# Queueing side work behind each slot's ELU, and making three weight tiles of the second MoE in place

## The chip, the cores and the metric

The kernel runs on one core of one Trainium2 chip. The metric is device time in microseconds (us) of one launch. Before the change the median of three runs is 1340.48 us (1339.67 to 1345.49).

## The reference, cut to what matters

Three layers follow each other: attention with pooled keys and values (8 batches, 8 heads, 576 queries of 64), a first MoE block with ELU (4608 tokens, 512 to 2048 to 512), and a second one with SoLU and a layer norm (512 to 1024 to 512).

```python
k_p = k.reshape(B, H, Sp, 8, D).mean(axis=3); v_p = ...          # pooled by 8
x = softmax(q @ k_p.T / 8) @ v_p                                  # 4608 x 512
h = x @ w_in                                                      # 512 -> 2048
g = np.where(h > 0.0, h, np.exp(np.minimum(h, 0.0)) - 1.0)        # ELU
x = g @ w_out                                                     # 2048 -> 512
h = x @ w_in2                                                     # 512 -> 1024
solu = h * softmax(h)
out = ((solu - mean) / sqrt(var + 1e-6) * g_ln) @ w_out2          # 1024 -> 512
```

## The kernel before

Every float32 operand of a matmul is split into a rounded high part and a low remainder, and three products (high by high, low by high, high by low) are added; the high part is a copy on ScalarE (ACT), the remainder a subtraction on VectorE (DVE). The weights come as 64-bit words and are converted by bit operations on ACT and DVE. A scheduler orders the instructions of each engine by when it believes they can run; the source's order decides among those that are ready.

The first MoE works on nine blocks of 512 tokens, in two ways.

Blocks 0, 1 and 2 are **three passes** of 16 *slots* (the loop over `slots`, j for the block, f for 128 columns of the hidden layer). A slot holds 12 matmuls of `m_h1` (line 529, into a bank `h`), ELU on ACT and DVE (`m_h1` lines 534 and 535 for the exponentials, `m_elu` line 541 on DVE, the copy `gh` at 545, the remainder `gl` at 552), and 12 matmuls of `m_o1` (line 564) for the slot before. Side work is sown into the slots: attention for later blocks (`att_half`, four steps for each *unit*, a pair of heads of one batch: scores 173, their maximum and difference 189 and 198, exponentials 203, sums 212 to 214, the multiplication on GpSimd 216, transposes 228 and 233 on TensorE, the product 252), and from block 1 on the *combinations* of the weights (`combo_in`, `combo_out`, the generator `todo`), which make sums of quarters of the weights for the third stage: DVE subtractions at 469, ACT copies at 474, remainders at 478, writes to DRAM (`w1d`, `w3d`) at 481. The tiles `ci` and `co` of the combinations, the blocks `xh`, `xl` and, later, the `sP`, `sA`, `sV`, `sS` tiles share six buffers (tag "x").

Blocks 3 to 8 are **three pairs**. Seven products of half size (Strassen in Winograd's form) replace eight. A pair has an *h stage* of 8 k by 7 steps (`h_step`, matmuls at 649) and an *o stage* of 7 by 4 steps (`mul_o`, matmuls at 739, operands by `g_op`: copy 729, remainder 730; sums by `g_sum` 723). `sx_build` loads and splits the inputs of a pair (loads at 596, splits at 604 and 605, sums at 616 to 632). Weights come through a ring of 14 buffers (`w_ring`, line 641, 256 KB each), read back from `w1d` and `w3d`. The results of `elu` lie in eight tiles `g11` to `g22` in the buffers of tag "w".

In the **last pair** the weights of the second MoE are made: `prep_load` (384) loads 512 KB, `prep_in` converts it into `F` (391 to 394), makes differences in `G` (422), splits seven results (428, 429) into a tile of tag "cv", which has two buffers, and writes each to DRAM (`w2d`, 430). `fetch` (441, 444) reads them back, 1 MB each, into the tiles that the products of the last stage use (`prod`, line 819): B11, B21 and T1 into the pool `pm`, the others into tag "w". All loads and stores are issued by SyncE's queue (SP), in its order.

The lines on which the order of this work rests before the change:

```python
            while credit > 0.999 and step < goal[j]:
                att_half(step)
...
            while quota >= 1:
                next(todo, None)
...
                if s == 0:
                    p2_load(0)
                    for n in ("B11", "B21", "T1"):
                        fetch(n)
```

## Time and profile before

| | |
|---|---|
| median of three runs | 1340.48 us (1339.67 to 1345.49) |
| the profiled execution | 1343.38 us, span 1341.5 us |
| TensorE busy | 1278.1 us (95%) |
| DVE, ACT, GpSimd busy | 988.0, 778.7, 185.8 us |
| DMA | 236.05 MB |
| mean granted TensorE clock | 0.987 |

The profile gives the busy time of each engine, for each idle stretch what ended it, and the clock that TensorE was granted (1.00 is 2.4 GHz). A matmul's record is longer than its place in the pipeline, so records of matmuls in a row overlap, and the idle time in front of one starts at the end of the record before. Lines are those of the kernel before.

### The profile page before, as it was taken

The page shows a single profiled execution, that of the slowest core. Times are in us where ns is not written, and L with a number is a line of the kernel's source. Part 1 is how long each engine was busy: PE and PEld are TensorE (multiplying, and loading weights), DVE is VectorE, ACT ScalarE, POOL GpSimd, SP SyncE. Part 2 cuts the span into 40 slices and gives each one's busy share as a digit, 9 for nine tenths or more (in the row PEclk, how much of TensorE's full clock was granted, in tenths as well). Part 3 has the DMA queues.
Part 4 walks back from the last instruction along what each step waited for, and adds up shares of the span by engine and source line. Part 5 has one row for each costly group of instructions (what it writes and reads, how often), then busy time and mean ns, then how long its engine had stood idle before and what let it go on. Part 6 is the DMA issues. An engine that isn't in the chain of part 4 may idle for free.

```text
span 1341.5 us, 17404 instructions
## 1 busy us (share of the span) xinstructions
PE 1278.1 (95%) x5972; PEld 1017.6 (76%) x5972; DVE 988.0 (74%) x1529; ACT 778.7 (58%) x1370; POOL 185.8 (14%) x150
## 2 busy tenths in 40 slices
PE   5889899899999999999999999899999999999998
PEld 4667677677777787777888777777788888888886
DVE  7798899986656789856796577974857575757563
ACT  4778565565556685537764368733645454545453
POOL 3445323332320001100000000000000010000000
PEclk9799999999999999999999999999999999999999
DMA  8578377773329877787666779989111111111001
GB/s 266 168 233 272 108 251 244 238 265 122 104 86 312 244 228 222 228 284 217 208 197 205 266 254 305 359 306 333 42 63 48 39 41 63 48 34 45 32 17 40
DMA packets 143272, 236.05 MB, mean 176 GB/s; under 512 B 13520, under 2 KB 61136, under 8 KB 141776
## 3 DMA queue, kind: packets, MB, share of 16 engines
q1 hardware_dynamic: 143184, 234.93, 53.9%
q8 instruction: 48, 0.79, 0.2%
q14 instruction: 40, 0.33, 0.1%
HBM read 168.82 MB, written 66.06 MB: 175 GB/s over the span
## 4 chain that ended last, share of the span: by engine, by line
PE 64%; DVE 7%; DMA 6%; ACT 2%; issue 2%; POOL 0%; SPq 0%; POOLq 0%; DVEq 0%; ACTq 0%
PE po L906 14%; PE hA L649 12%; PE oA L739 11%; PE x L819 7%; PE z L819 3%; PE o L564 2%; PE pt L891 2%; PE h L529 2%; PE hB L649 2%; PE oB L739 2%; PE y L819 2%; DMA raw<-in_w 1%; PE at L252 1%; PE at L173 1%; DMA x1d<-xo 1%
## 5 line engine op out<-in xcount | busy, mean ns | idle before, releaser
L906 PE MATMUL po<-w,dhl 128*128 128x512 f32 x864 | 208.1, 394 | 0.4 <-ACT dhl L894 0.4
L739 PE MATMUL oA<-op,wr 128*128 128x512 f32 x864 | 203.9, 394 | 3.3 <-DMA wr<-w3d 3.2
L739 PEld LDWEIGHTS oA<-op,wr 128*128 128x128 f32 x864 | 162.1, 189 | 41.7 <-issue 6.5
L906 PEld LDWEIGHTS po<-w,dhl 128*128 128x128 f32 x864 | 161.1, 188 | 34.7 <-ACT dhl L894 0.7
L729 ACT CAST op<-g 128x1024 fp32r<-128x1024 f32 x84 | 88.2, 1051 | 79.5 <-PE oA L739 59.0
L730 DVE TENSOR_TENSOR op<-g,op 128x1024 fp32r<-128x1024 f32 x84 | 102.6, 1234 | 32.9 <-ACT op L729 32.8
L649 PE MATMUL hA<-sS,wr 128*128 128x512 f32 x432 | 111.1, 396 | 5.3 <-ACT sp L661 3.8
L881 POOL TENSOR_TENSOR sc<-sc,mhalf 128x1 f32<-128x1 f32 x36 | 25.4, 705 | 602.0 <-DVE sc L880 332.6
L452 POOL TENSOR_TENSOR wol<-wo,woh 128x512 fp32r<-128x512 f32 x48 | 81.3, 1694 | 172.1 <-ACT woh L451 172.0
L649 PEld LDWEIGHTS hA<-sS,wr 128*128 128x128 f32 x432 | 79.7, 188 | 27.2 <-ACT sp L661 6.2
L819 PE MATMUL x<-w,xh 128*128 128x512 f32 x272 | 97.2, 399 | 0.9 <-ACT sn L827 0.9
L869 DVE TENSOR_REDUCE sc<-hb 128x1 f32<-128x1024 f32 x18 | 21.9, 1219 | 94.8 <-ACT hb L855 94.2
L216 POOL TENSOR_TENSOR es<-es,sm 128x720 f32<-128x720 f32 x28 | 44.6, 1592 | 316.1 <-DVE sm L214 125.7
L564 PE MATMUL o<-gh,woh 128*128 128x512 f32 x192 | 79.7, 415 | 2.9 <-ACT gh L545 2.8
L529 PE MATMUL h<-xh,wh 128*128 128x512 f32 x192 | 79.6, 414 | 0.0
L564 PE MATMUL o<-gh,wol 128*128 128x512 f32 x192 | 77.0, 401 | 1.7 <-POOL wol L452 1.7
L529 PE MATMUL h<-xh,wl 128*128 128x512 f32 x192 | 76.2, 397 | 0.4 <-POOL wl L375 0.4
L909 ACT ACTIVATE ot<-po,sc 128x512 f32<-128x512 f32 x36 | 24.7, 685 | 88.8 <-PE po L906 54.6
L529 PE MATMUL h<-xl,wh 128*128 128x512 f32 x192 | 76.2, 397 | 0.0
L669 DVE SCALAR_TENSOR_TENSOR g<-ep,g 128x512 f32<-128x512 f32 x72 | 50.0, 705 | 25.8 <-ACT ep L668 25.7
L723 DVE TENSOR_TENSOR g<-g,g 128x1024 f32<-128x1024 f32 x48 | 60.8, 1291 | 0.1
L819 PEld LDWEIGHTS x<-w,xh 128*128 128x128 f32 x272 | 51.1, 188 | 12.6 <-ACT sn L827 1.8
(329 smaller groups left out, 2811.1 us busy)
## 6 DMA issues: line engine op xcount, KB each, us to landing
wr<-w1d SPq DMA_DIRECT2D x168, 256.0 KB
wr<-w3d SPq DMA_DIRECT2D x168, 256.0 KB
raw<-in_w SPq DMA_DIRECT2D x48, 512.0 KB
v<-in_v SPq DMA_DIRECT2D x32, 288.0 KB
x1r<-x1d SPq DMA_DIRECT2D x9, 1024.0 KB
out<-ot SPq DMA_DIRECT2D x36, 256.0 KB
w1d<-ci SPq DMA_DIRECT2D x16, 512.0 KB
w3d<-co SPq DMA_DIRECT2D x16, 512.0 KB
```

The lines of the kernel that those rows point to most:

```text
L216: n = eng.tensor_tensor(es, es, bc(sm, NG), op=ALU.mult)
L452: nc.gpsimd.tensor_tensor(ol, t[:, f % 4, :], oh.bitcast(F32), op=ALU.subtract)
L529: nc.tensor.matmul(h[:, 0:n], a[g][:, kk, fo:fo + P], x[j][:, kk, 0:n], start=(i == 0), stop=(i == 3 * KDM - 1))
L564: nc.tensor.matmul(acc, a[:, dm * P:(dm + 1) * P], x[:, 0:n], start=(f == 0 and m == 0), stop=(f == NF - 1 and m == 2))
L649: nc.tensor.matmul(bank, w[:, a, kk], x[:, b, kk], start=(start and m == 0), stop=(stop and m == 5), skip_group_check=True,)
L669: nc.vector.scalar_tensor_tensor(d, e, 1.0, h, op0=ALU.subtract, op1=ALU.max)
L723: nc.vector.tensor_tensor(d, x, y, op=op)
L729: nc.scalar.copy(o[:, 0], src)
L730: nc.vector.tensor_tensor(o[:, 1], src, o[:, 0].bitcast(F32), op=ALU.subtract)
L739: nc.tensor.matmul(banks[d], ws[i][:, a, d * P:(d + 1) * P], o[:, b, i], start=(start and t == 0 and i == 0 and m == 0), stop=(stop and t ...
L819: nc.tensor.matmul(bank, x[:, o:o + P], w[:, y + k, :], start=(start and m == 0), stop=(stop and m == 5), skip_group_check=True,)
L906: nc.tensor.matmul(po, a[:, c, :], w[c // 4][:, c % 4, :], start=(m == 0), stop=(m == 3 * NC2 - 1))
```

## The change

Four things change. In blocks 1 and 2 the combinations and the attention steps are traced under `tc.issue_after(gate["elu"])`, which puts each of their DVE instructions behind the newest ELU (`m_elu`) on DVE; instructions on other engines are not bound by it. The eight `g` tiles are allocated together, in another order, so that the eight fetched weights that follow them in tag "w" fall on other buffers. B11, T1 and B21 of the second MoE are split straight into their `pm` tiles, without the write to `w2d` and without the fetch; `pm` opens earlier, `G` is half as large. And the last nine of the 26 pieces of `prep_load` and `prep_in` move from the h stage of the last pair into its o stage, one for each step, while the fetches are spread over steps 3, 4 and 6.

```diff
@@ prep_in
-            for o, x, y in ((t1, b12, b11), (t3, b22, b12), (t2, b22, t1), (t4, b21, t2)):
-                nc.vector.tensor_tensor(o, x, y, op=ALU.subtract)
+            sub(G[:, 0], b12, b11)
+            sub(G[:, 1], b22, b12)
+            sub(b12, b22, G[:, 0])
             return
+        if step == 6:
+            sub(G[:, 0], b21, b12)
...
-            t = sb.tile([P, 2, 512], F32R, name="cv2", tag="cv", bufs=2)
+            here = n in ("B11", "T1", "B21")
+            if here:
+                if a == 0:
+                    w2[n] = pm.tile([P, 4, 512], F32R, name="w2", tag="m", bufs=3)
+                t = w2[n][:, a:a + 3:2]
+            else:
+                t = sb.tile([P, 2, 512], F32R, name="cv2", tag="cv", bufs=2)
             nc.scalar.copy(t[:, 0], w)
             nc.vector.tensor_tensor(t[:, 1], w, t[:, 0].bitcast(F32), op=ALU.subtract)
...
@@ h_step
-            if k % 4 == 0:
-                for q in (11, 12, 21, 22):
-                    G.setdefault(q, [None, None])[k // 4] = sb.tile([P, 4, 512], F32, name=f"g{q}", tag="w", bufs=8)
+            if k == 0:
+                for q in (11, 21, 22, 12):
+                    G[q] = [sb.tile([P, 4, 512], F32, name=f"g{q}", tag="w", bufs=8) for _ in range(2)]
@@ slots
-                att_half(step)
+                with tc.issue_after(gate["elu"]) if j > 0 else ExitStack():
+                    att_half(step)
...
-            while quota >= 1:
-                next(todo, None)
-                quota -= 1
+            if j > 0:
+                with tc.issue_after(gate["elu"]):
+                    while quota >= 1:
+                        next(todo, None)
+                        quota -= 1
@@ last pair
+        late = extra[-9:] if last else []
+        extra = extra[:len(extra) - len(late)]
...
+                if late:
+                    late.pop(0)()
...
-                    for n in ("B11", "B21", "T1"):
-                        fetch(n)
-                if s == 4:
-                    fetch("T2")
-                    fetch("T3")
+                for n in {3: ("T2", "T3"), 4: ("T4", "B22"), 6: ((0, 0), (0, 1), (1, 0), (1, 1))}.get(s, ()):
+                    fetch(n)
                 if s == 5:
-                    for n in ("T4", "B22", (0, 0), (0, 1)):
-                        fetch(n)
                     p2_split(0)
```

The order of TensorE's instructions stays but for a few neighbours. Three places on other engines show the change; line numbers of the changed kernel are 8 higher in the slots and the pairs.

DVE in block 1, around the ELU of the slot whose hidden bank is `h_1821` (before):

```order
L478 TENSOR_TENSOR co<-co 128x512 x2
L492 TENSOR_TENSOR ci<-wh,wl 128x512 x2
L469 TENSOR_TENSOR ci<-ci 128x256 x4
L541 SCALAR_TENSOR_TENSOR e<-e,h_1821 128x512
L478 TENSOR_TENSOR ci<-ci 128x512 x2
L552 TENSOR_TENSOR gl__1843<-e,gh 128x512
L189 TENSOR_REDUCE mx_1871<-at 128x6
```

The same place now:

```order
L560 TENSOR_TENSOR gl__1791<-e,gh 128x512
L486 TENSOR_TENSOR ci<-ci 128x512
L549 SCALAR_TENSOR_TENSOR e<-e,h_1821 128x512
L477 TENSOR_TENSOR co<-wo 128x256 x2
L477 TENSOR_TENSOR co<-wo,co 128x256
L560 TENSOR_TENSOR gl__1843<-e,gh 128x512
L477 TENSOR_TENSOR co<-wo,co 128x256
L189 TENSOR_REDUCE mx_1871<-at 128x6
```

Between two slots stood eight instructions of combinations ahead of the ELU, now one; the combinations that came early in block 1 now go on to the end of block 2.

ACT at the end of block 2, before: the last two slots have the banks `h_3559` and `h_3609`, `sS` belongs to the split of the first pair's inputs.

```order
L534 ACTIVATE e<-h_3559 128x512
L535 ACTIVATE e<-e 128x512
L545 CAST gh<-e 128x512
L451 CAST woh<-wo 128x512
L604 CAST sS_3697<-su 128x1024
L534 ACTIVATE e<-h_3609 128x512
L535 ACTIVATE e<-e 128x512
L545 CAST gh<-e 128x512
```

The same place now:

```order
L542 ACTIVATE e<-h_3559 128x512
L543 ACTIVATE e<-e 128x512
L553 CAST gh<-e 128x512
L459 CAST woh<-wo 128x512
L482 CAST co<-co 128x512 x2
L612 CAST sP_3603<-sP_3603 128x1024
L542 ACTIVATE e<-h_3609 128x512
L543 ACTIVATE e<-e 128x512
L612 CAST sA_3605<-sA_3605 128x1024
L612 CAST sV<-su 128x1024
L553 CAST gh<-e 128x512
```

The splits of `sP`, `sA` and `sV`, which stood four and more slots earlier, now stand around the last slot's exponentials; `sP` and `sA` are loaded behind the last writes of `ci`, since the six buffers of tag "x" are in use until then.

SP in the o stage of the last pair, before (`x1r` is the first block for the last stage):

```order
L783 DMA x1r_7953<-x1d 128x4x512
L430 DMA w2d<-cv_7825 128x2x512
L430 DMA w2d<-cv_7854 128x2x512
L441 DMA w_7955<-w2d 128x2048
L441 DMA w_7957<-w2d 128x2048
L441 DMA w_7959<-w2d 128x2048
L641 DMA wr<-w3d 128x512 x8
```

The same place now:

```order
L791 DMA x1r_7917<-x1d 128x4x512
L649 DMA wr<-w3d 128x512 x11
L441 DMA w2d<-cv_7986 128x2x512
L649 DMA wr<-w3d 128x512
L441 DMA w2d<-cv_8011 128x2x512
L649 DMA wr<-w3d 128x512 x3
L441 DMA w2d<-cv_8015 128x2x512
```

Behind `x1r` eleven ring loads follow at once; the writes of `w2d` now wait inside the ring loads of steps 3 and 4, and the three fetches are gone.

## Rows read from the trace of the kernel before

**Rows 1.** The page: busy time by engine, and one of the costliest groups.

```profile
PE 1278.1 (95%) x5972; PEld 1017.6 (76%) x5972; DVE 988.0 (74%) x1529; ACT 778.7 (58%) x1370; POOL 185.8 (14%) x150
...
L739 PE MATMUL oA<-op,wr 128*128 128x512 f32 x864 | 203.9, 394 | 3.3 <-DMA wr<-w3d 3.2
```

**Rows 2.** Timeline of the last pair, TensorE; the first is the chain's.

```profile
709.97 16.34 PE oA L739 x72
...
783.62 1.66 PE L649 MATMUL hA<-sS,wr 128*128 128x512 f32 x6 [0.76 <-ACT sp L661]
...
803.70 1.52 PE L649 MATMUL hA<-sP,wr 128*128 128x512 f32 x6
...
843.38 1.66 PE L649 MATMUL hA<-sS,wr 128*128 128x512 f32 x6 [1.61 <-ACT sp L661]
...
873.47 56.27 PE L739 MATMUL oA<-op,wr 128*128 128x512 f32 x240 [3.15 <-DMA wr<-w3d]
```

**Rows 3.** Windows: blocks 1 and 2, from one result store to the next.

```profile
core 0: us, PE busy (x) PEld busy (x) DVE busy (x) ACT busy (x) POOL busy (x), PEclk, DMA share, GB/s
168.90:291.30 122.40, 114.07 (x570) 89.47 (x569) 117.38 (x199) 74.43 (x155) 38.82 (x22) 1.00 0.75 244
291.30:401.20 109.90, 106.39 (x528) 82.81 (x527) 68.69 (x102) 63.83 (x126) 29.34 (x21) 1.00 0.41 127
```

**Rows 4.** Timeline of block 1, TensorE: instructions with idle time before them.

```profile
216.32 0.60 PE L228 MATMUL pt<-ident,es 128*72 128x128 f32 x4 [1.92 <-DVE es L198]
...
268.36 0.60 PE L228 MATMUL pt<-ident,es 128*72 128x128 f32 x4 [1.50 <-ACT xr L266]
```

**Rows 5.** Timeline before the first of these waits: ACT and DVE.

```profile
208.39 0.63 ACT L535 ACTIVATE e<-e 128x512 f32<-128x512 f32 x1
...
209.86 2.51 DVE L469 TENSOR_TENSOR ci<-ci 128x256 f32<-128x256 f32 x4
...
212.30 0.68 DVE L541 SCALAR_TENSOR_TENSOR e<-e,h 128x512 f32<-128x512 f32 x1
```

**Rows 6.** Windows: the last pair's h stage from 775, o stage, a stretch.

```profile
775.00:851.50 76.50, 71.82 (x303) 55.55 (x302) 62.12 (x99) 60.77 (x106) 0.00 (x0) 1.00 0.88 294
851.50:929.60 78.10, 74.95 (x323) 61.28 (x322) 56.90 (x60) 33.70 (x42) 0.00 (x0) 0.98 0.94 334
870.00:880.00 10.00, 6.85 (x24) 5.26 (x23) 10.00 (x10) 2.28 (x3) 0.00 (x0) 0.83 1.02 385
```

**Rows 7.** Timeline of SP, and the chain: fetches and the load behind them.

```profile
859.30 2.37 SPq L441 DMA_DIRECT2D w<-w2d  x3
...
861.78 11.56 DMA wr<-w3d
```

**Rows 8.** Chain and timeline of the last pair: a load, a conversion's step.

```profile
775.63 6.79 DMA raw<-in_w
...
829.57 0.69 DVE L393 SCALAR_TENSOR_TENSOR F<-raw,F 128x512 uint32<-128x512 uint32 x1
```

**Rows 9.** Chain (two loads) and timeline at the end of block 2.

```profile
372.52 3.21 DMA sA<-x0d
...
378.31 3.61 DMA su<-x0d
...
379.39 1.04 ACT L604 CAST sP<-sP 128x1024 fp32r<-128x1024 f32 x1
...
391.22 0.69 DVE L541 SCALAR_TENSOR_TENSOR e<-e,h 128x512 f32<-128x512 f32 x1 [0.38 <-ACT e L535]
...
396.10 0.59 ACT L534 ACTIVATE e<-h 128x512 f32<-128x512 f32 x1
```

**Rows 10.** Timeline: GpSimd's remainder of the output weights, two of them.

```profile
207.12 4.98 POOL L452 TENSOR_TENSOR wol<-wo,woh 128x512 fp32r<-128x512 f32 x1 [4.99 <-ACT woh L451]
...
223.57 1.29 POOL L452 TENSOR_TENSOR wol<-wo,woh 128x512 fp32r<-128x512 f32 x1 [1.54 <-ACT woh L451]
```

**Rows 11.** Waits of DVE by pair: us, instructions, longest in us.

```profile
DVE e L541 <- ACT e L535: 18.4, 13, 3.0
```

More of the change, by code (lines that the diff above doesn't have):

```diff
@@ L413, in prep_in @@
             if step == 0:
-                st["F"], st["G"] = (pg.tile([P, 4, 512], F32, name=t, tag="fg", bufs=2) for t in "FG")
+                st["F"] = pg.tile([P, 4, 512], F32, name="F", tag="f", bufs=1)
+                st["G"] = pg.tile([P, 2, 512], F32, name="G", tag="g", bufs=1)
             prep_conv(8 + 4 * (step % 2) + 2 * (step // 2) + a, st["F"][:, step])
@@ L418, in prep_in @@
         b11, b12, b21, b22 = (F[:, i] for i in range(4))
-        t1, t2, t3, t4 = (G[:, i] for i in range(4))
+        sub = lambda o, x, y: nc.vector.tensor_tensor(o, x, y, op=ALU.subtract)
         if step == 4:
-            for o, x, y in ((t1, b12, b11), (t3, b22, b12), (t2, b22, t1), (t4, b21, t2)):
-                nc.vector.tensor_tensor(o, x, y, op=ALU.subtract)
+            sub(G[:, 0], b12, b11)
+            sub(G[:, 1], b22, b12)
+            sub(b12, b22, G[:, 0])
             return
+        if step == 6:
+            sub(G[:, 0], b21, b12)
         for n, w in (
-            (("B11", b11), ("T1", t1)), (("T2", t2), ("B21", b21)), (("T3", t3), ("T4", t4)), (("B22", b22),)
+            (("B11", b11), ("T1", G[:, 0])), (("T2", b12), ("B21", b21)), (("T3", G[:, 1]), ("T4", G[:, 0])), (("B22", b22),)
         )[step - 5]:
-            t = sb.tile([P, 2, 512], F32R, name="cv2", tag="cv", bufs=2)
+            here = n in ("B11", "T1", "B21")
[5 more added lines that the diff above has]
+                t = sb.tile([P, 2, 512], F32R, name="cv2", tag="cv", bufs=2)
             nc.scalar.copy(t[:, 0], w)
             nc.vector.tensor_tensor(t[:, 1], w, t[:, 0].bitcast(F32), op=ALU.subtract)
-            nc.sync.dma_start(
-                out=w2d[:, W2[n]].rearrange("p (h a) f -> p h a f", a=2)[:, :, a], in_=t.bitcast(F32)
-            )
+            if not here:
+                nc.sync.dma_start(
+                    out=w2d[:, W2[n]].rearrange("p (h a) f -> p h a f", a=2)[:, :, a], in_=t.bitcast(F32)
+                )
     def fetch(n):
-        if n in ("B11", "B21", "T1"):
-            t = pm.tile([P, 4, 512], F32R, name="w2", tag="m", bufs=3)
-        else:
-            t = wtile("w2")
+        t = wtile("w2")
         if n in W2:
@@ L540, in m_elu @@
         e, h = gt[j, f]
-        nc.vector.scalar_tensor_tensor(
+        gate["elu"] = nc.vector.scalar_tensor_tensor(
             e[:, 0:n], e[:, 0:n], 1.0, h[:, 0:n], op0=ALU.subtract, op1=ALU.max
-        )
+        ).ins
         gh = p1.tile([P, 512], F32R, name="gh", tag="gh")
@@ L1127 @@
             att.close()
+            pm = ctx.enter_context(tc.tile_pool(name="pm", bufs=3, side="right", reuse_waits="tile"))
             att2 = ExitStack()
@@ L1160 @@
         w_ring(("o", 0, 7))
-        if last:
-            att2.close()
-            pm = ctx.enter_context(tc.tile_pool(name="pm", bufs=3, side="right", reuse_waits="tile"))
         g_op(0, 2)
@@ L1189 @@
                         credit -= 1.0
+                if late:
+                    late.pop(0)()
             o_done(c, s)
+            if last and s == 2:
+                att2.close()
             if s == 4:
```

2 lines of the change are left out of this document (removed).

## The prediction, as recorded before the changed kernel ran

> **What bounds the kernel now.** The page comes first: TensorE is busy for 1278.1 of 1341.5 us, 95% [rows 1]. So the change can only be worth the time in which TensorE stands, and what standing costs besides. A matmul's record lasts 394 ns, yet 72 in a row take 16.34 us, 0.227 us each [rows 1, 2]. A wait starts where the last record ends, so 0.394 − 0.227 = 0.17 us of filling is lost beside it, and six matmuls behind a wait take 1.66 us where six without one take 1.52 [rows 2]: 0.14 more. A wait of w us therefore costs about w + 0.3.
>
> Then the windows, since the average hides the stages. Block 1 takes 122.40 us with DVE busy for 117.38, block 2 takes 109.90 with DVE at 68.69 [rows 3]. The two do much the same matmuls; block 1 is where the combinations run early. TensorE stands for 122.40 − 114.07 = 8.33 us in block 1 and for 109.90 − 106.39 = 3.51 in block 2. I count eight waits of over 0.2 us in the first and five in the second, so they lose 8.33 + 8 × 0.3 = 10.7 and 3.51 + 5 × 0.3 = 5.0 us.
>
> What is late there is read one step back. Two of block 1's large waits are transposes of attention, on DVE's difference (1.92 us) and on ACT's output copy (1.50) [rows 4]. Ahead of the first, ACT's exponentials had ended at 208.39 + 0.63 = 209.02, while DVE's ELU began at 212.30: four combinations of 2.51 us lay between [rows 5]. An ELU late by 3.3 us makes `gh`, `gl` and all side work behind it late.
>
> In the last pair I read three things. From 775 on its h stage stands for 76.50 − 71.82 = 4.68 us, its o stage for 78.10 − 74.95 = 3.15 [rows 6]. The latter is a single wait, for a ring buffer at 873.47, and the clock around it is 0.83 [rows 2, 6]. SP had issued the three fetches at 859.30, and the ring load behind them took 11.56 us [rows 7]; a load of 512 KB elsewhere in this pair took 6.79 [rows 8].
>
> **The change part by part.**
>
> *1. Block 1's ELU comes first.* The eight combinations between two slots become one, so the ELU no longer sits behind 2.51 us. At best all 10.7 us go. At worst none do: DVE's 117.38 us are only spread. I take 6.5, some three fifths, because part of the waits have attention's own chain behind them (the copy `xr` on ACT), which no order on DVE shortens. **−6.5 (−10.7 to 0).**
>
> *2. Block 2 gets what block 1 loses.* If DVE's work is shared evenly, each pass has (117.38 + 68.69) / 2 = 93 us in some 112, or 83%. That is far from the 96% of block 1, but above the 63% of block 2 now. No gain is to be had there, as DVE only gets more. The upper end is half of block 1's loss, 5.4. I take 2, nearer to the row of block 2. **+2 (0 to +5.4).**
>
> *3. The end of block 2.* The inputs of the first pair use the buffers that the combinations give back, and the copies of `sP`, `sA` and `sV` now stand around the last slot's exponentials. Before, `sP` was copied at 379.39, in 1.04 us, and the last exponentials began at 396.10 [rows 9]. The last combinations now run behind the ELU at 391.22 of the slot before. With two DVE instructions of 0.69 behind it, they end at 393.3; a load takes 3.21 to 3.61 [rows 9], so it lands at 396.5 to 396.9. If ACT meets that copy first, the exponentials begin at 396.9 + 1.04 = 397.9, late by 1.8, and two more copies ahead of `gh` add 2 × 1.04 less the 0.7 of the ELU that lies beside them: 1.4. The sum is 3.2. The lower end is nothing, if the load is early; the upper is a whole load and two copies with nothing beside them, 3.61 + 2.08 + 0.3 = 6.0. **+3 (0 to +6.0).**
>
> *4. The ring's wait in the last pair.* Three fetches (3 MB) leave, and eleven ring loads follow the first block's load at once. The wait is 3.15 us, and the 240 matmuls behind it take 56.27 where 240 × 0.227 = 54.5 would do [rows 2], 1.8 more, for which I hold the clock of 0.83. **−4.9 (−4.9 to 0)**; the full value, since nothing else stands in front of the ring now but writes of 512 KB.
>
> *5. The last pair's h stage.* It loses 4.68 us and seven times 0.3, 6.8. Nine of the 26 pieces of preparation leave it, those at its end, where the largest wait is (1.61 us on ACT's `sp` at 843.38; one near its start is 0.76) [rows 2]. I take under half. **−3 (−6.8 to 0).**
>
> *6. The o stage takes those nine pieces.* They are three conversions of three DVE instructions, four subtractions and seven remainders: 20 instructions of at most 0.69 us [rows 8], 13.8 us beside the 56.90 that DVE works in 78.10 [rows 6]; ACT has more room. They fit, 70.7 of 78.1, but each can put off a remainder of `op`, and one raw load now stands behind the ring. At worst its 6.79 us show whole. **+1 (0 to +6.8).**
>
> I cost the other edits at nothing. The `g` tiles in another order only decide which fetch waits for which step; the cover is the third stage's own use of the fetched tiles, which comes after the o stage. If it is gone, a fetch shows, and the raw load bounds it. One subtraction goes to another tile, none is added. `pm` opens earlier and nothing waits for it.
>
> Sum: −6.5 + 2 + 3 − 4.9 − 3 + 1 = **−8.4 us** (ends −22.4 and +18.2). The profiled execution took 1343.38 us, 2.9 above the median of 1340.48. It becomes 1335.0, and a median of **1332.1**.
>
> A rule speaks against this. In block 1 GpSimd's remainder `wol` took 4.98 us once and 1.29 another time, for the same tile [rows 10]; the longer one began at 207.12 and spans the four combinations of [rows 5]. The Trainium skill, "SBUF — State Buffer", section "Who interferes with whom", says that DVE and GpSimd share a pair of ports as an exclusive lock, and that a DVE instruction with two inputs in SBUF and a GpSimd instruction that reads SBUF block each other for the whole instruction. The trace agrees, with 4.98 beside 1.29. By the rows' stretching alone, and with these combinations still beside GpSimd but in other places, the sum stays; by the rule at its hardest it is the last rival below.
>
> **The rivals.**
>
> *Both passes come out clean.* Terms 1, 2, 5 and 6 at their good ends, of 5 only 5.0 us: −10.7 + 0 + 3 − 4.9 − 5 + 0 = −17.6, so **1323**. For it speaks that block 2 at 63% loses only 5.0; against it, that the waits on `xr` are on ACT.
>
> *The waits are only spread.* Half of block 1's loss goes and comes back in block 2, and the late raw load shows: −5.4 + 5.4 + 3 − 4.9 − 3 + 6.8 = +1.9, so **1342**. So the change would not do what it says. For it speaks that the same instructions stay on the same engine; against it, the 40 us that DVE has free in block 2.
>
> *Attention waits behind an ELU that itself waits* (the other side). An attention step that could run must now stand behind the newest ELU, and DVE's ELU waited 13 times for ACT's exponentials, 18.4 us in all, 1.42 each [rows 11]. A maximum behind it is late by 0.68 + 1.42, and TensorE by 0.3 more: 2.4 us per unit. Twelve units fall in the two passes. With half of them it is +14.4 in place of terms 1 and 2; with +3 of term 3 and −6.9 of the rest, +10.5, so **1351**. From five units on it is slower by 0.5%. Against it: between a maximum and its transposes lie a whole slot's 24 matmuls, 5.5 us.
>
> *GpSimd's multiplication is held up.* If the combinations now stand beside the attention's multiplication on GpSimd in block 2, as they stood beside `wol`, six of these are longer by 4.98 − 1.29 = 3.7 [rows 10], and 0.3 for TensorE: 6 × 4.0 = 23.9, so −8.4 + 23.9 = +15.5, **1356**. The rule of the Trainium skill named above would have it so. Against it: in block 1 the multiplications had the same neighbours, and the waits there were on DVE and ACT.
>
> **How the numbers follow.** Half a per cent, 6.7 us, is about what a measurement can tell from no change: below 1333.8 is faster, above 1347.2 slower. Chances: the forecast (1332, own range 1326 to 1337) 0.44; both clean 0.18; spread 0.24; attention behind the ELU 0.09; GpSimd 0.05. The forecast's case lies below 1333.8 in two thirds (0.30), clean wholly (0.18), spread in a quarter (0.06): faster 0.54. The rest of these three is no change, 0.33 after 0.01 for a tail; slower is 0.13, the two last cases but for a little of them. The range leaves out those two and the tails of the clean and the spread case: 1319 to 1344.
>
> **What would show it.** Blocks 1 and 2 should take about 116 and 112 us, with DVE near 93 in each, and no transposes waiting on `es` or `xr` by 1.5 us. At the end of block 2 TensorE waits on `gh`, `gl` or `sP` by some 3 us more. Around 870 the ring's wait is gone and the clock is 1.00. The h stage from 775 stands for under 3 us, and no remainder of `op` makes the o stage wait. The prediction is wrong if block 2 loses what block 1 gains, if a transpose waits on GpSimd's product, if the ring waits elsewhere (behind the writes to `w2d`, or the raw load), or if a fetch late in the o stage meets the start of the third stage.

## The result, and the profile after

The changed kernel takes 1320.18 us (median of 6 runs, 1317.58 to 1323.19), the kernel before 1342.78 (6 runs, 1339.67 to 1346.35). The ratio is 0.9831 (0.9808 to 0.9855): 22.7 us faster, with 19.5 to 25.8 as the interval's ends. The forecast was 8.4. The direction was right and the time lies inside the range, near its lower end; the size is off by a factor of 2.7. So the question is which term of the sum was too small.

The page first: one line, the busy time of TensorE, in a span of 1316.7 us. It is busy 9.8 us less than in [rows 1], while the span is 24.8 shorter; the rest is standing time.

```profile
PE 1268.3 (96%) x5972; PEld 1013.0 (77%) x5972; DVE 973.1 (74%) x1529; ACT 779.7 (59%) x1370; POOL 186.1 (14%) x150
```

The windows of the changed kernel: the end of block 0, and blocks 1 and 2 from one result store to the next, as in [rows 3].

```profile
core 0: us, PE busy (x) PEld busy (x) DVE busy (x) ACT busy (x) POOL busy (x), PEclk, DMA share, GB/s
124.00:158.67 34.67, 33.44 (x164) 25.85 (x163) 22.47 (x33) 22.07 (x43) 12.90 (x9) 1.00 0.29 87
158.67:269.07 110.40, 110.36 (x557) 87.67 (x556) 90.11 (x156) 69.08 (x142) 37.22 (x22) 1.00 0.69 217
269.07:381.71 112.64, 109.11 (x549) 85.94 (x548) 91.62 (x157) 71.58 (x144) 33.92 (x21) 1.00 0.63 195
```

Block 1 has gone from 122.40 to 110.40 us, and TensorE stands in it for 0.04 us where it stood for 8.33. DVE is evened out to 90.11 and 91.62 us, close to the 93 of the forecast. Block 2 is 2.7 us longer.

Windows that end at a store compare stretches that aren't quite alike: block 2's window now holds 21 more records of matmuls, since a few of the next pair and of attention go ahead of the last results. A sharper measure is the same instruction in both traces. The table gives the *lead* of a kernel over the one before: the time of an instruction on ACT in the trace of before, less its time in the other trace. The marks are ACT's first exponential of slots 12, 16, 33 and 47 (counted from 0), the first copy of an operand `op` in the first pair and the last one in the second, the eleventh copy `sn` of the last stage, and the end of the last matmul. The columns hold what the lead gains from mark to mark, and the sum.

```
                 start   blk 0   blk 1   blk 2   to the   pairs   last   last    all
                 to 12   12-16   16-33   33-47   o stage  1, 2    pair   stage
changed kernel    +5.9    +4.3   +12.0    -1.0    -1.6    -3.6    +9.0   -0.2   24.8
combinations      +3.0    +2.7   +11.7    -2.3    -3.1    +0.2    -1.5   +0.1   10.9
attention         +2.2    +2.7    +5.1    +1.2    -0.8     0.0    +1.3   -0.1   11.5
both (slots)      +4.2    +4.3   +12.0    -0.8    -1.4    -1.0    -0.4   +0.1   16.9
last pair only    +2.7    -0.2    +0.8    -1.6    +0.4    -1.3    +7.5   -0.1    8.1
```

(The lower four rows belong to experiments below.) The columns of slots 12 to 16 and 16 to 33 are the same to 0.1 us in the changed kernel and in the one with both slot edits: +4.3 and +12.0. The first column isn't the change's. Up to slot 12's exponentials ACT does the same instructions in the same order in both kernels, and so does DVE but for one combination that starts 0.43 us ahead of them in the trace before; the lead stands at 3.8 us at the very first slot already: the granted clock was 0.55 in 30 to 45 us of the trace before, and 0.89 in that of the changed kernel.

```profile
30.00:45.00 15.00, 14.62 (x52) 8.84 (x53) 11.66 (x18) 11.44 (x23) 2.61 (x3) 0.55 0.54 152
```

```profile
30.00:45.00 15.00, 13.55 (x69) 8.84 (x65) 13.12 (x18) 14.01 (x26) 3.28 (x3) 0.89 0.63 178
```

The first of these windows is of the kernel before, the second of the changed one. The −3.6 of the first two pairs is of the same kind: in 572 to 580 us, at the start of the second pair, the changed kernel's clock was 0.57, and that of the kernel before 1.00. So one profile against one other holds some 4 us of chance; the verdicts below go by medians and ratios, and the table says where.

**Where block 0 gained.** This place isn't in the prediction. The timelines of the kernel before, around slot 12, show DVE, ACT and TensorE:

```profile
135.13 2.32 DVE L492 TENSOR_TENSOR ci<-wh,wl 128x512 f32<-128x512 f32 x2
137.38 4.48 DVE L469 TENSOR_TENSOR ci<-ci 128x256 f32<-128x256 f32 x3
141.78 0.74 DVE L148 TENSOR_REDUCE kr<-k 128x72 f32<-128x576 f32 x1
142.44 0.67 DVE L541 SCALAR_TENSOR_TENSOR e<-e,h 128x512 f32<-128x512 f32 x1
...
137.08 0.61 ACT L535 ACTIVATE e<-e 128x512 f32<-128x512 f32 x1
...
144.50 1.04 PE L228 MATMUL pt<-ident,es 128*72 128x128 f32 x4 [2.76 <-ACT late L262]
```

ACT's exponentials ended at 137.08 + 0.61 = 137.69. The ELU that needed them began at 142.44, 4.75 us later: five combinations and a step of attention stood ahead of it in DVE's queue, three of the five and the step not yet finished. TensorE stood for 2.76 us. The source gives out combinations from block 1 on, but the scheduler had drawn the first of them, which depend on weights only, forward into block 0. Now the ELU runs as soon as ACT is done (a wait of 2.52 us on ACT, with nothing in front):

```profile
131.83 0.69 DVE L549 SCALAR_TENSOR_TENSOR e<-e,h 128x512 f32<-128x512 f32 x1 [2.52 <-ACT e L543]
```

The cost there was more than the wait. The granted clock fell there, and the matmul records behind the wait, which last 0.39 us elsewhere, took 0.63:

```profile
140.00:150.00 10.00, 7.24 (x29) 5.63 (x28) 9.91 (x14) 4.74 (x11) 1.57 (x2) 0.83 0.38 115
```

**Waits of TensorE after.** The timeline of the changed kernel: two instructions with idle time before them that follow each other in this respect (none lies between them), then the larger ones of block 2, of its end and of the last pair's later part.

```profile
129.23 0.50 PE L572 MATMUL o<-gl__1114,woh 128*128 128x512 f32 x1 [1.23 <-DVE gl__1114 L560]
...
303.98 0.39 PE L233 MATMUL pr<-ident,es 128*72 128x128 f32 x2 [0.83 <-DVE es L198]
...
356.56 0.50 PE L572 MATMUL o<-gh,woh 128*128 128x512 f32 x1 [1.30 <-ACT gh L553]
...
378.61 0.50 PE L572 MATMUL o<-gh,woh 128*128 128x512 f32 x1 [0.91 <-ACT gh L553]
...
385.45 0.60 PE L228 MATMUL pt<-ident,es 128*72 128x128 f32 x4 [1.43 <-DVE es L198]
...
392.79 0.97 PE L657 MATMUL hA<-sP,wr 128*128 128x512 f32 x3 [2.15 <-DMA wr<-w1d]
...
768.05 1.20 PE L657 MATMUL hA<-sA,wr 128*128 128x512 f32 x4 [1.12 <-ACT sp L669]
...
823.40 0.73 PE L747 MATMUL oA<-op,wr 128*128 128x512 f32 x2 [1.48 <-DVE g L717]
```

From 129.23 to 303.98, some 175 us, TensorE doesn't stand for a time that the timeline shows. The waits on `es` and on `xr` of [rows 4] are both gone. Block 2 now waits for `gh`, by 1.30 and, at its end, 0.91 (term 3); behind it a transpose of attention waits for `es` by 1.43 (1.18 before), and a ring load of the first pair is late by 2.15. In the last pair the ring's wait is gone, and TensorE waits for a sum into `g` where the o stage starts, 1.48.

### The profile page after: what moved, and what is told of

The parts are those of the page before. It is cut to its first block, busy times and chain, and to the rows that moved or that the text cites. A ratio compares the mean times of both kernels' runs of the same rounds, so it can differ in the third digit from the quotient of the medians.

```text
span 1316.7 us, 17373 instructions
## 1 busy us (share of the span) xinstructions
PE 1268.3 (96%) x5972; PEld 1013.0 (77%) x5972; DVE 973.1 (74%) x1529; ACT 779.7 (59%) x1370; POOL 186.1 (14%) x150
## 4 chain that ended last, share of the span: by engine, by line
PE 73%; DVE 11%; DMA 7%; ACT 5%; issue 2%; POOL 0%; SPq 0%; POOLq 0%; DVEq 0%; ACTq 0%
PE po L914 14%; PE hA L657 11%; PE oA L747 10%; PE x L827 7%; PE o L572 7%; PE h L537 7%; PE z L827 3%; DMA raw<-in_w 3%; PE pt L899 2%; PE at L173 2%; PE at L252 2%; PE hB L657 2%; PE y L827 2%; PE pt L228 2%; PE oB L747 2%
## 5 line engine op out<-in xcount | busy, mean ns | idle before, releaser
L738 DVE TENSOR_TENSOR op<-g,op 128x1024 fp32r<-128x1024 f32 x84 | 102.9, 1231 | 26.2 <-ACT op L737 25.8
L889 POOL TENSOR_TENSOR sc<-sc,mhalf 128x1 f32<-128x1 f32 x36 | 22.3, 618 | 596.4 <-DVE sc L888 323.4
L460 POOL TENSOR_TENSOR wol<-wo,woh 128x512 fp32r<-128x512 f32 x48 | 84.2, 1754 | 150.7 <-ACT woh L459 150.7
L669 ACT COPY sp<-hA 128x512 f32<-128x512 f32 x72 | 41.5, 583 | 38.6 <-PE hA L657 38.3
```

Of the source, the lines that this page charges most:

```text
L460: nc.gpsimd.tensor_tensor(ol, t[:, f % 4, :], oh.bitcast(F32), op=ALU.subtract)
L669: nc.scalar.copy(t, bank)
L738: nc.vector.tensor_tensor(o[:, 1], src, o[:, 0].bitcast(F32), op=ALU.subtract)
```

## The experiments

Each was timed against the kernel before on the same chip; the first four together. "The changed kernel" is the whole change.

### Which edit of the slots gives it, and what the last pair gives

The theory after the result: most of the gain is the combinations', in block 1 and in block 0's last slots. The rivals: attention's place does as much, or the last pair gave most. Only the combinations behind the newest ELU:

```diff
+                with tc.issue_after(gate["elu"]):
+                    while quota >= 1:
+                        next(todo, None)
```

> Only the combinations stand behind the newest ELU; attention and the last pair are as before. Theory A (the gain is mostly the combinations': late ELUs of block 1 and of the last slots of block 0, into which some of them had been drawn): 13 to 15 us faster than before, block 1 near 111 us and the last four slots of block 0 some 4 us shorter. Theory B (the attention steps' place matters as much): 5 to 8 us faster. Theory C (the last pair gave most of it): at most 8 us faster.

Only the attention steps:

```diff
+                with tc.issue_after(gate["elu"]) if j > 0 else ExitStack():
+                    att_half(step)
```

> Only the attention steps stand behind the newest ELU. Theory A: within 3 us of before, since the ELU still waits for combinations. Theory B: 5 to 10 us faster. Theory D (an attention step behind an ELU that waits is late itself): 2 to 10 us slower.

Both, with the last pair as before:

> Both kinds of side work stand behind the newest ELU, the last pair is as before. Theory A: 14 to 16 us faster than before, the same as with the combinations alone within 2 us. Theory B: 4 us or more better than the better one of the two alone. Theory C: 10 us faster or less.

The rest of the change alone, that is the changed kernel with those two edits undone:

```diff
-                with tc.issue_after(gate["elu"]) if j > 0 else ExitStack():
-                    att_half(step)
+                att_half(step)
```

> Only the second MoE's part of the change (weights made in place, order of the g tiles, late pieces, moved fetches); the slots are as before. Theory A: 6 to 9 us faster than before, of which the ring's wait is 5. Theory C: 12 us faster or more. If 22 us of the whole change were partly luck of the clock at the start, this and the slots alone would add up to 17 or less.

| | median us | ratio to before | us |
|---|---|---|---|
| combinations alone | 1332.91 | 0.9926 (0.9901 to 0.9952) | −9.9 |
| attention alone | 1335.17 | 0.9944 (0.9922 to 0.9966) | −7.5 |
| both | 1327.68 | 0.9896 (0.9872 to 0.9921) | −14.0 |
| last pair alone | 1335.07 | 0.9943 (0.9921 to 0.9965) | −7.7 |

(The last column is the ratio's distance from 1, times the 1342.6 us of before.) The slots and the last pair add up to 21.7, the 22.7 of the whole within the intervals, so the lucky start of the profile has no part in the median. The theory fell in three points: the combinations alone were to give 13 to 15 us and give 9.9, attention alone was to give less than 3 and gives 7.5, and the two together, 14.0, are 4.1 better than the combinations alone, where 2 was the most. So the rival that attention's place counts too was right, though not that it counts as much in block 1 (+5.1 against +11.7 in the table). The last pair didn't give most. Together the two give less than their sum of 17.4; block 1's loss can be taken away only once. The windows of block 1, in the kernel with the combinations alone and in the one with attention alone:

```profile
163.08:273.86 110.78, 110.41 (x558) 87.67 (x556) 95.69 (x156) 69.15 (x142) 33.07 (x22) 1.00 0.67 215
```

```profile
163.49:280.04 116.55, 112.99 (x559) 89.12 (x558) 111.72 (x198) 75.68 (x154) 40.42 (x22) 0.99 0.82 258
```

With the combinations held back, block 1 is clean (0.37 us of standing). With attention held back alone, DVE is still busy for 111.72 of 116.55 us, yet TensorE stands for 3.56 instead of 8.33. That is against the prediction's reading, by which the waits followed DVE's share. Why does the combinations' kernel still end 4 us behind the one with both? The table of leads says: it loses 2.3 in block 2 and 3.1 after it (both edits: 0.8 and 1.4), and gains 1.6 less in block 0. In block 2 a transpose waits there for attention's difference, and at the block's end `gh` is late by more:

```profile
308.70 0.60 PE L228 MATMUL pt<-ident,es 128*72 128x128 f32 x4 [1.46 <-DVE es L198]
...
384.63 0.50 PE L564 MATMUL o<-gh,woh 128*128 128x512 f32 x1 [1.66 <-ACT gh L545]
```

The kernel with both waits 0.90 and 0.70 at these places. Why attention's place does this isn't shown.

In the kernel with attention alone one wait is on GpSimd, as the prediction's last rival had it, though in block 1: a multiplication on GpSimd took 4.45 us, where most take 1.39, while six combinations ran on DVE.

```profile
253.33 4.45 POOL L216 TENSOR_TENSOR es<-es,sm 128x720 f32<-128x720 f32 x1 [0.89 <-DVE sm L214]
...
257.84 0.81 PE L228 MATMUL pt<-ident,es 128*72 128x128 f32 x4 [2.04 <-POOL es L216]
```

A quantity that could explain block 1 in all of these kernels is how late the ELUs run: the start of the ELU on DVE less the end of ACT's second exponential, summed over the 16 slots of block 1 from the timelines' rows.

```
                                 ELUs of block 1   lead gained
                                 late by, us       16 to 33, us
before                           24.3                0
kept out of block 0 (below)      12.4               +2.3
attention alone                  12.2               +5.1
combinations alone                5.5              +11.7
changed kernel                    5.0              +12.0
subtractions twice (below)        4.7               +9.8
```

It sorts the kernels roughly, into those that gain most of block 1's loss and those that don't, and not finely: 12.4 and 12.2 go with 2.3 and 5.1. Outside block 1 it fails. The same sum over block 2 is 6.0 before, 8.6 in the changed kernel and 15.4 with the subtractions done twice, which costs 0.7 us there; a run at the end makes the ELUs of block 0 less late and is slower.

### Place or order: the combinations kept out of block 0 alone

Here they may not start ahead of block 0's last ELU, but run as early as they can in blocks 1 and 2.

```diff
+        if j == 0:
+            gate["elu0"] = gate["elu"]
...
+                with tc.issue_after(gate["elu0"]):
+                    while quota >= 1:
+                        next(todo, None)
```

> Only this: the combinations may not start ahead of the last ELU of block 0; inside blocks 1 and 2 they run as early as before. Theory E (what counts is that no side work stands ahead of an ELU that could run): the last slots of block 0 are 3 to 4 us shorter, block 1 keeps its waits or gets more of them, as what was drawn forward now runs there; 0 to 4 us faster than before. Theory F (it was enough to take them out of block 0): 9 us faster or more, as with the combinations behind each ELU.

1338.05 us, 0.997 (0.9952 to 0.9989): 4.0 faster. The lead gains 4.2 us in slots 12 to 16, just as with the whole change, and 2.3 in block 1, as theory E had it. In block 1 TensorE still waits, as three rows of its timeline show:

```profile
198.32 0.60 PE L228 MATMUL pt<-ident,es 128*72 128x128 f32 x4 [1.26 <-ACT xr L266]
...
228.20 0.60 PE L228 MATMUL pt<-ident,es 128*72 128x128 f32 x4 [1.36 <-DVE es L198]
...
269.25 0.60 PE L228 MATMUL pt<-ident,es 128*72 128x128 f32 x4 [1.57 <-DVE es L198]
```

So block 0's part is worth 4 us by itself, and the rest of the slots' gain needs the order inside block 1.

### DVE's share or the order: subtractions done twice

```diff
         for o, x, y in ((t1, b12, b11), (t3, b22, b12), (t2, b22, t1), (t4, b21, t2)):
             nc.vector.tensor_tensor(o, x, y, op=ALU.subtract)
+            nc.vector.tensor_tensor(o, x, y, op=ALU.subtract)
             yield
```

> The changed kernel with each of the four subtractions of a combination done twice (the same result again): some 32 us more work for DVE in blocks 1 and 2, which brings its share there from 82% to about 95%, that of block 1 before the change. Theory L, that of the prediction (the waits follow DVE's share): blocks 1 and 2 lose about 10 us each, 1335 to 1340 us in all. Theory E (they follow what stands ahead of the ELU): blocks 1 and 2 stay within 2 us each, 1320 to 1324.

1325.17 us, 0.9874 (0.9847 to 0.9900): 16.9 faster than before, 5.8 us slower than the changed kernel by the ratios, between the two expectations and nearer to theory E (the excess of 1.2 us over its upper end is within the interval). The windows of blocks 1 and 2 show which one holds:

```profile
162.33:274.94 112.61, 110.70 (x560) 87.90 (x558) 105.23 (x188) 68.52 (x141) 39.22 (x22) 1.00 0.67 213
274.94:388.32 113.38, 109.86 (x545) 84.95 (x544) 105.59 (x187) 70.51 (x143) 34.11 (x21) 1.00 0.62 194
```

DVE now works for 93% of both blocks, 29 us more than in the changed kernel, and block 1 costs 2.2 us more, block 2 0.7. Before the change 96% went with 8.33 us of standing; here 93% goes with 1.91. The ELUs of block 1 are late by 4.7 us, as few as in the changed kernel. So it is the order that takes block 1's loss away, and DVE's share costs little up to here. That a higher share would cost nothing isn't shown, and of the 5.8 us that this run is slower the two blocks account for 2.9. What in the order does it isn't separated either: the change keeps combinations from running several slots ahead of their place, and by that it also thins out what stands ahead of each ELU; no run does one without the other.

### The ring's wait alone

The kernel before, with only the three fetches moved from behind step 0 to behind step 3:

```diff
                 if s == 0:
                     p2_load(0)
+                if s == 3:
                     for n in ("B11", "B21", "T1"):
                         fetch(n)
```

> As before, but the fetches of B11, B21 and T1 stand behind step 3 of the last o stage and not behind step 0. Theory A4 (the ring's wait and the clock behind it are these three fetches): 4 to 5 us faster, no wait on a ring buffer near 870. Its rival (the ring is late for another reason, or the fetches only hit later ring loads): within 2 us of before, with a wait on a ring buffer in a later step.

1338.45 us, 0.9970 (0.9955 to 0.9984): 4.0 us faster. Three windows of 20 us around the place of [rows 2, 7]: the kernel before, this one, and the changed one.

```profile
865.00:885.00 20.00, 16.85 (x68) 13.48 (x67) 20.00 (x20) 6.24 (x6) 0.00 (x0) 0.91 1.02 389
```

```profile
865.00:885.00 20.00, 20.00 (x90) 16.54 (x89) 19.72 (x20) 7.38 (x7) 0.00 (x0) 1.00 0.89 305
```

```profile
845.00:865.00 20.00, 20.00 (x90) 16.57 (x89) 19.80 (x22) 8.59 (x11) 0.00 (x0) 1.00 0.92 312
```

The wait and the fall of the clock are gone in both. The term of 4.9 had its cause right, and nearly its size: the fetches' place alone does it, without making anything in place.

### The late pieces

The changed kernel with all 26 pieces in the h stage:

```diff
-        late = extra[-9:] if last else []
+        late = []
```

> The changed kernel with all 26 pieces of preparation in the last pair's h stage, none late. If the late pieces are worth the 3 us less 1 us that the prediction gave them: 2 us slower than the changed kernel, with waits on the copies of the hidden banks at the end of the h stage. If they cost as much as they save: the same within 1 us.

1326.10 us, 0.9889 (0.9862 to 0.9916). It was run a second time, beside another run:

> The changed kernel with no late pieces once more, beside the run above on the same chip, to size the nine late pieces. The prediction's terms 5 and 6 come to 2 us; the first run without late pieces gave 5. If the late pieces are worth 5: this is 4 to 6 us above the changed kernel's time. If the 5 were chance: 1 to 3.

1325.10 us, 0.9874 (0.9847 to 0.9900). Against the changed kernel's 0.9831, the two are 0.58% and 0.43% slower, 7.8 and 5.8 us, with intervals that reach some 4 us to either side; against the run with the g tiles reordered (next), which gave 0.9845 on the chip of the first, it is 5.9. That is about 6 us, three times the 2 of terms 5 and 6. But the size is loose: the six times of each of the two runs spread over 9 us and leave a gap of 4.3 and 5.6 us between the third and the fourth, where the median falls. The profiles can say more, since each holds the last pair apart from the rest. From the first matmul of its h stage to the last one of its o stage, as these windows have it for the kernel before and for the changed one, the pair takes 171.6 and 161.9 us.

```profile
758.10:929.70 171.60, 160.95 (x674) 126.95 (x673) 133.39 (x172) 100.99 (x155) 0.00 (x0) 0.98 0.88 306
```

```profile
742.10:904.00 161.90, 156.13 (x674) 124.64 (x673) 132.44 (x172) 99.87 (x155) 0.00 (x0) 1.00 0.85 287
```

Several of the kernels here have the same last pair, so the table takes their mean. The o stage is counted from its first matmul.

```
last pair, us                    h stage   o stage   both    profiles, lowest to highest
as in the kernel before            87.1      84.2    171.3   5, 169.3 to 173.0
the three fetches moved alone      89.4      80.0    169.4   1
as in the changed kernel           83.0      80.7    163.7   6, 161.9 to 167.9
no late pieces                     84.9      82.1    166.9   2, 165.3 and 168.5
thirteen late pieces               86.4      82.2    168.6   1
```

By this the late pieces are worth 3.2 us and the whole change of the pair 7.6, near the 7.7 of its own run. So the nine pieces are worth 3 to 6 us, above the forecast's 2 and not well sized. The h stage swings by several us in kernels whose last pair is the same (81.3 to 87.3 among the six); the o stage doesn't (80.6 to 80.8). One wait of the last pair without late pieces is larger than any that the changed kernel has there:

```profile
766.61 2.93 PE L657 MATMUL hA<-sS,wr 128*128 128x512 f32 x6 [2.38 <-ACT sp L669]
```

The records behind it are long (2.93 us for six matmuls, 1.66 after other waits), and the clock was 0.72 in 766 to 772 us. It stands in the first third of the h stage and not at its end, as the expectation had it, and a kernel with the late pieces has 1.90 there (the one with 3.2 pieces, below), so this wait alone doesn't show what they do. Thirteen late pieces instead of nine (the buffers of preparation, `att2`, are then closed behind step 3 and not step 2):

```diff
-        late = extra[-9:] if last else []
+        late = extra[-13:] if last else []
```

> The changed kernel with 13 of the 26 pieces late where it has 9. If every piece that leaves the h stage saves there what nine did by the run without late ones, about 0.5 us each, and the o stage has room: 1 to 2 us faster than the changed kernel. If the o stage is full, or the first fetches now wait: 1 to 4 us slower, with waits on op or on a fetched tile.

1325.91 us, 0.9868 (0.9840 to 0.9895): no gain, rather 5 us lost against the changed kernel. The wait at the start of the o stage, 1.48 us on `g` at 823.40, is 2.02 now:

```profile
831.66 0.76 PE L747 MATMUL oA<-op,wr 128*128 128x512 f32 x2 [2.02 <-DVE g L717]
```

That is 0.5 us and not 5. The clock fell behind it (0.76 in 831 to 838), and the o stage is 1.5 us longer than the changed kernel's; the rest stands in the h stage, which swings that much without any change.

### The order of the g tiles

```diff
-                for q in (11, 21, 22, 12):
+                for q in (11, 12, 21, 22):
```

> The changed kernel with the g tiles allocated in the order 11, 12, 21, 22, as before. If the order costs nothing, as predicted: the same as the changed kernel within 1 us. If the fetches otherwise wait for tiles that are read late: 2 to 6 us slower, with waits on fetched tiles at the start of the last stage.

1321.10 us, 0.9845 (0.9819 to 0.9870): the same as the changed kernel within the measurement. The prediction's nothing holds.

### The end of block 2, and attention in block 0

These three were also tries at a faster kernel. More pieces for half a slot, so that the last combinations come earlier:

```diff
-            quota += 2.6 * (j > 0)
+            quota += 3.0 * (j > 0)
```

> The changed kernel with 3.0 pieces of combinations for half a slot where it has 2.6, so that the last are done four slots earlier. If the loss at the end of block 2 (a copy gh and a ring load that are late) comes from the last combinations, as in step 3 of the prediction: 1.5 to 3 us faster than the changed kernel. If it comes from the splits alone or the denser work makes ELUs late: no change or up to 3 us slower.

1319.89 us, 0.9835 (0.9808 to 0.9862), the same as the changed kernel. The trace shows two effects that cancel, by the leads. Between slot 47 and the first o stage nothing is lost (changed kernel: 1.6), and the ring load is late by 0.47 us and not 2.15:

```profile
388.67 1.63 PE L657 MATMUL hA<-sP,wr 128*128 128x512 f32 x6 [0.47 <-DMA wr<-w1d]
```

In block 1 the lead gains 10.1 instead of 12.0, with small waits of attention on `xr` and `es`. So only block 2 was made denser:

```diff
-            quota += 2.6 * (j > 0)
+            quota += (0, 2.6, 3.2)[j]
```

> The changed kernel with 3.2 pieces of combinations for half a slot in block 2 alone (2.6 in block 1, as there). If the run with 3.0 in both gained 1.6 us or more at the end of block 2 and lost 2 in block 1 to the denser pieces there: block 1 as in the changed kernel, the first pair starts 1.5 to 3 us earlier, 1.5 to 2.5 us faster than the changed kernel. If the end of block 2 depends on the splits of the first pair's inputs instead, or block 2 gets its own waits from the denser pieces: no change or up to 2 us slower.

1325.04 us, 0.9867 (0.9846 to 0.9888): 5 us slower than the changed kernel, more than either expectation had. Block 1 gains 12.0 as it should, but blocks 2 and its end lose 2.5 and 2.6 (changed kernel: 1.0 and 1.6), so the denser pieces bring their own lateness, as the second expectation had it; a conversion of the first pair is waited for instead of the ring:

```profile
396.46 1.19 PE L657 MATMUL hB<-sP,wr 128*128 128x512 f32 x4 [1.62 <-DVE sP L613]
```

And the last pair, which this edit doesn't touch, gains 2.4 and not 9.0 in this profile, so part of the 5 us can be the last pair's chance. Last, attention behind the newest ELU in block 0 too:

```diff
-                with tc.issue_after(gate["elu"]) if j > 0 else ExitStack():
+                with tc.issue_after(gate["elu"]) if "elu" in gate else ExitStack():
```

> The changed kernel with the attention steps behind the newest ELU in block 0 too. Theory E: 1 to 4 us faster than the changed kernel, as TensorE still waits there. Its rival (block 0 waits for the conversion of the weights and not for attention): no change, or slower by 1 to 3 us, as attention becomes late.

1324.42 us, 0.9871 (0.9846 to 0.9895): slower than the changed kernel. The lead gains 2.4 us in slots 12 to 16 instead of 4.3, where TensorE meets a new wait:

```profile
132.71 0.79 PE L572 MATMUL o<-gh,woh 128*128 128x512 f32 x1 [2.12 <-ACT gh L553]
```

The ELUs of block 0 are late by 11.7 us in sum here and by 19.5 in the changed kernel. So a less late ELU isn't enough by itself: the rival's slowdown came, and what makes `gh` late there wasn't taken apart.

None of these beats the changed kernel.

## Why the prediction was right in sign and wrong in size

By its own terms, with the slots' and the last pair's medians where a run has them apart and the leads inside a profile otherwise:

```
term                                  forecast     measured
block 0's last slots                    none        -4.0  (run of its own)
1  block 1's ELU comes first            -6.5       -12.0  (lead, 16 to 33; to 32: -10.3)
2  block 2 gets what block 1 loses      +2          +1.0  (lead, 33 to 47)
3  end of block 2                       +3          +1.6  (lead, to the o stage)
   slots, sum                           -1.5       -14.0  (run of its own)
4  ring's wait                          -4.9        -4.0  (run of its own)
5, 6  late pieces                       -2          -3 to -6  (two runs, profiles; loose)
   last pair, sum                       -6.9        -7.7  (run of its own)
```

That the ELU stood behind the combinations was right, and so was the ring's wait; the sum of the slots wasn't. The step that failed is term 1, "Block 1's ELU comes first": 6.5 us were forecast, 12.0 measured, and 4.0 more came ahead of block 1, where the prediction put nothing. Three faults lie behind it.

First, the value: the prediction had the whole 10.7 us as its lower end and took 6.5, "because part of the waits have attention's own chain behind them (the copy `xr` on ACT), which no order on DVE shortens". All of it went, the waits on `xr` too. With the combinations alone behind the ELU, block 1 stands for 0.37 us in all. ACT works in its own order, and ahead of the copy `xr` of [rows 4] stood other work that waited for DVE's combinations:

```profile
266.76 0.62 ACT L474 CAST ci<-ci 128x512 fp32r<-128x512 f32 x1 [3.37 <-DVE ci L469]
267.28 0.62 ACT L535 ACTIVATE e<-e 128x512 f32<-128x512 f32 x1
267.81 0.68 ACT L266 COPY xr<-at 128x320 f32<-128x320 f32 x2
```

The copy of a combination waited for 3.37 us, and the second exponential and `xr` behind it; ahead of the other wait on `xr` in block 1, at 247.14, it was a copy `gh` that waited for a late ELU (2.54 us). The name at the end of a wait was ACT's, its cause DVE's order. The upper end itself was well placed: the lead gains 10.3 us by slot 32, where block 2 begins, and 1.7 more in that slot (20.5 and 22.2 us of lead at slots 32 and 33), where a transpose had waited for `es` by 1.28 us at 294.56. (The 10.7 counts eight waits of over 0.2 us; the trace has seven, and four and not five in block 2, so 10.4 and 4.7.)

Second, the place: the term stopped at block 1. The combinations' first instructions stood in block 0, ahead of the ELU of slot 12, which was 4.75 us late. The windows of the prediction began at 168.90, and it shows no view of block 0; the trace of the kernel before has the rows, without any run of the change. That was 4 us.

Third, the yardstick for term 2, "If DVE's work is shared evenly, each pass has ... 93 us in some 112, or 83%. That is far from the 96% of block 1", took DVE's share as what the waits follow, and so charged block 2 for its fuller queue. The share came out as forecast, but subtractions done twice gave 93% in both blocks at 2.2 and 0.7 us, and attention alone at 111.72 of 116.55 us took away half the standing. Up to there the order on DVE counts, and not how much DVE does. Term 2's +1.0 is near its +2 by luck: the reason doesn't hold, and counted from slot 32, block 2 loses nothing but gains 0.7.

The last pair's sum was right within the interval (7.7 against 6.9). Its parts are less sure: the ring's wait gave 4.0 of the forecast 4.9 (4.2 in the o stage of the table by stages), the late pieces 3 to 6 instead of 2. With the 3.2 of the profiles the two come to 7.2 to 7.4, near the 7.7. The h stage from the place of [rows 6] on stands for 3.46 us in the changed kernel, against 4.68 before and the "under 3" that was to show it, and the wait at the o stage's start is in it. The pair's own column in the table swings by several us between kernels whose last pair is the same (+9.0 in the changed kernel, +6.2 with the g tiles reordered, +2.4 with 3.2 pieces in block 2). Some of that is the clock at the start of the pair: in 742 to 757 us it was 0.77 in the second run without late pieces and 1.00 in the changed kernel.

```profile
742.00:757.00 15.00, 11.98 (x40) 9.02 (x40) 9.77 (x9) 5.16 (x6) 0.00 (x0) 0.77 0.64 213
```

```profile
742.00:757.00 15.00, 12.69 (x53) 9.06 (x52) 13.54 (x14) 6.18 (x10) 0.00 (x0) 1.00 0.75 259
```

So how the late pieces and the fetches share the last pair's gain is known to a few us only.

The rivals: "both passes come out clean" (1323) was the nearest, and right of block 1; with block 0's 4 us its 17.6 would have been 21.6, of the 22.7 measured. "The waits are only spread" fell with block 1's 0.04 us of standing. "Attention waits behind an ELU that itself waits" fell with the run of attention alone, 7.5 us faster. "GpSimd's multiplication is held up" fell for the changed kernel: its multiplications take 46.0 us in all, 44.6 before, the longest in blocks 1 and 2 takes 2.91, and the one wait of TensorE on them there is 0.16 us. That the thing exists the kernel with attention alone shows (4.45 us, and 2.04 of waiting); that is near the size that the rival gave it, once and not six times. The Trainium skill, "SBUF — State Buffer", section "Who interferes with whom", has DVE and GpSimd share a pair of ports as an exclusive lock. The 4.45 us beside combinations agree with it; no run here tests it by itself. DVE's combinations took less time after the change than before, as these groups show (three of the six that there are; 120 to 401 us; before, then after).

```profile
L469 DVE TENSOR_TENSOR ci<-ci 128x256 f32<-128x256 f32 x32 | 18.7, 613 | 0.0
L478 DVE TENSOR_TENSOR ci<-ci 128x512 fp32r<-128x512 f32 x16 | 14.5, 921 | 0.2
L492 DVE TENSOR_TENSOR ci<-wh,wl 128x512 f32<-128x512 f32 x16 | 12.9, 815 | 0.0
```

```profile
L477 DVE TENSOR_TENSOR ci<-ci 128x256 f32<-128x256 f32 x32 | 14.4, 473 | 0.0
L486 DVE TENSOR_TENSOR ci<-ci 128x512 fp32r<-128x512 f32 x16 | 11.8, 742 | 0.4
L500 DVE TENSOR_TENSOR ci<-wh,wl 128x512 f32<-128x512 f32 x16 | 10.7, 683 | 0.0
```

The same instructions take 46.1 us before and 36.9 after; the other three groups take 28.7 and 29.0. The two sets meet GpSimd at other times; whether that is the difference was not tried.

## What to carry to other kernels

When an instruction that feeds the bound engine stands in one queue with side work, look at what stands ahead of it and how long after its input is ready it starts, slot by slot; here the queue's busy share said little, up to 93%. That lateness finds the place to look at; it doesn't price it. A scheduler can draw side work that depends on nothing still to come forward, out of the place where the source puts it, so the loss is looked for ahead of that place too. A wait that ends on one engine can have its cause two queues back: ask what that engine was itself waiting for before counting it as out of reach.

## What the runs showed of the hardware

A wait of TensorE could cost more than its length and the filling of 0.3 us: behind the 2.76 us at 144.50 the clock was 0.83 over 10 us, and slots 12 to 16 lost 4.3 us where the wait was 2.76. After waits at the start of a pair the clock fell in some runs (0.77) and not in others (1.00), and the clock at the program's start differed as well (0.55 and 0.89 in the same 15 us, with the same order); differences of 2 to 4 us between two single profiles are therefore no evidence. The same 128x256 subtraction on DVE took 613 ns on the mean in one arrangement and 473 in another, and the same multiplication on GpSimd 1.39 us mostly and 4.45 once, with combinations on DVE beside it.
